# Group 1's keys and queries: four loads of four tokens a packet on half the partitions each, or two loads of two tokens a packet on all of them

## The chip, the cores and the metric

The kernel runs on one core of a Trainium2 chip. A core has a matrix engine (TensorE, PE in the profile), a vector engine (DVE), a scalar engine (ACT), a GpSimd engine (POOL) and a sync engine (SP), which work side by side and wait for one another by semaphores. SBUF is the on-chip memory of 128 partitions; PSUM is the matrix engine's output memory, cut into eight banks. Transfers between the device's main memory (HBM) and SBUF are issued by an engine's queue and carried out by 16 DMA engines. The metric is the device time of one execution in microseconds (us); lower is better.

## The reference

Two stages follow one another. The first is attention with a sliding window of 128 tokens and four sink tokens, for four sequences of 768 tokens, eight heads of 64 features:

```
scores = q @ k^T / 8                    # per sequence and head
keep   = (k_pos < 4) | (0 <= q_pos - k_pos < 128)
a      = softmax over the kept scores
x      = a @ v                          # put together to 3072 tokens x 512 features
```

The second is a gated feed-forward block on the 3072 tokens:

```
g   = x @ w_gate                        # 512 x 1536
out = (g * sigmoid(g) * (x @ w_val)) @ w_out   # 1536 x 512
```

The inputs and the output are float32; the kernel calculates in bfloat16 and adds up in float32.

## The kernel before, in words

The tokens are cut into twelve groups of 256, three to a sequence (`GC`). For each group the kernel brings keys and queries into SBUF, turns them so that the features lie on the partitions (`kTs` and `qTs`: head pair by head pair, 64 features of an even head above 64 of an odd one, tokens along the row), multiplies them to scores, takes exponentials on ACT, masks on DVE, multiplies with the values, divides by the sums, turns the result into `xT`, and feeds it to the feed-forward block. The attention of a later group is laid between the feed-forward products of an earlier one.

The order of the work on each engine is the order of the program's text: the schedule is written out by hand (`tc.manual_schedule()`), and every engine carries out its own instructions in that order. Nothing is planned by cost. What is moved in the text moves on its engine's queue.

How keys and queries get turned depends on the group. Group 0 comes in by two ways at once: heads 0 to 3 as float32 by the queues of SP and ACT (`st`, line 205) and then cast, heads 4 to 7 by POOL's queue, which casts on the way (`x0`, line 216). In `x0` each partition holds two neighbouring tokens of a head (`by_two`, line 198). Group 1, the one that the change touches, comes by four loads of POOL's queue (`load_rows`, line 97). Each takes 64 partitions: a partition holds four neighbouring tokens (`by_rows`, line 86, "r=4"), the even heads of the four pairs lie on partitions 0 to 63 and the odd ones on 64 to 127. So each load has 64 x 4 packets of 4 x 64 elements. Later groups come by whole token rows (`load_nat`).

The next work on POOL's queue, in the program's order, are the values of groups 0 and 1 (`va`, line 151, four loads), the first gate and value weights (`wg`, `wv`, line 162), and three small copies. All of these loads share the 16 DMA engines.

`step_T` (line 252) turns group 1 on the matrix engine. A matrix product with an identity matrix turns 64 tokens x 64 features. It uses a quarter of the array: partitions 0 to 63 give columns 0 to 63 (an even head), partitions 64 to 127 give columns 64 to 127 (an odd head), in turn. One call handles two head pairs with 16 such products into one PSUM bank; there are four calls, two for the keys and two for the queries (lines 820 to 823). After its 16 products each call copies its bank to `kTs` or `qTs`, on ACT or on DVE, and puts the four interleaved tokens back in order. The third call, the queries of pairs 0 and 1, is copied by DVE (line 271); the other three are copied by ACT (line 269).

Then come, on the matrix engine, the first eight products with group 0's values (`step_PV`, line 494), the scores of group 1 for pairs 0 and 1 (`step_S`, line 326), 16 more products with values, the scores of pair 2, the sinks' scores (line 432), the turning of group 0's result (line 543), the scores of pair 3, and then the first feed-forward product (`pg`, line 564). `step_S` for pairs 0 and 1 multiplies the second half of group 0's keys with the first half of group 1's queries first, then the first half of group 1's keys with all its queries, and last the second half with the second half.

Of the kernel before, what the change touches and what calls it, by code (L numbers as in the profile page):

```python
# [7 lines left out]
FP32 = mybir.dt.float32  # L8
BF16 = mybir.dt.bfloat16
# [5 lines left out]
def kernel(  # L15
# [12 lines left out]
    nc = tc.nc  # L28
    P = 128
    B, H, S, D = q.shape  # L30
# [8 lines left out]
    NP2 = H // 2  # L39
# [15 lines left out]
    def pool(name, bufs, psum=False):  # L55
        if psum:
            return ctx.enter_context(
                tc.tile_pool(name=name, bufs=bufs, space=bass.MemoryType.PSUM))
        return ctx.enter_context(tc.tile_pool(name=name, bufs=bufs))
# [3 lines left out]
    rowp = pool("rowp", 3)  # L63
# [16 lines left out]
    def bank(shape, dtype, name):  # L80
        return psum.tile(shape, dtype, tag="b", name=name)


    rows, nats, vas = {}, {}, {}

    def by_rows(src, b, w, pairs, t0):

        hs = slice(2 * pairs.start + w, 2 * pairs.stop, 2)
        return src[b, hs, t0:t0 + 256].rearrange("p (m r) d -> m p (r d)", r=4)

    ALL = slice(0, NP2)

    def new_rows(g):
        rows[g] = rowp.tile([P, 2, NP2, 4 * D], BF16, tag="rows", name="rows")
        return rows[g]

    def load_rows(g, i):
        b, c = divmod(g, GC)
        if g not in rows:
            new_rows(g)  # L100
        for w in range(2):
            nc.gpsimd.dma_start(  # L102
                rows[g][64 * w:64 * (w + 1), i],
                by_rows((k, q)[i], b, w, ALL, c * 256))

    def load_nat(g):
        b, c = divmod(g, GC)
# [65 lines left out]
    ident = const.tile([P, P], BF16)  # L173
# [21 lines left out]

    def by_two(src, h0, n=4):
        return src[0, h0:h0 + n, 0:256].rearrange("h (m r) d -> m h (r d)", r=2)

    x0 = const.tile([P, 2, H, 2 * D], BF16)
    st = [rowp.tile([P, H, 2 * D], FP32, tag="rows", name="st") for _ in range(2)]
    for h0 in (0, 2):
        for i, eng in ((0, nc.sync), (1, nc.scalar)):
            eng.dma_start(st[i][:, h0:h0 + 2], by_two((k, q)[i], h0, 2))
# [9 lines left out]
    for i in range(2):  # L215
        nc.gpsimd.dma_start(x0[:, i, 4:8], by_two((k, q)[i], 4))  # L216
    nc.gpsimd.iota(tq, [[1, P]], base=0, channel_multiplier=0,
                   allow_small_or_imprecise_dtypes=True)
    nc.gpsimd.iota(tk, [[0, 1]], base=0, channel_multiplier=1,
                   allow_small_or_imprecise_dtypes=True)  # L220
    load_rows(1, 0)
    load_rows(1, 1)
    load_v(0)
    load_v(1)
# [6 lines left out]
    kTs, qTs, es_t, e_t, xns, xTs = {}, {}, {}, {}, {}, {}  # L231
# [15 lines left out]
    def new_T(b):  # L247
        if b not in kTs:
            kTs[b] = kqtp.tile([P, NP2, S], BF16, tag="kT", name="kT")
            qTs[b] = kqtp.tile([P, NP2, S], BF16, tag="qT", name="qT")  # L250

    def step_T(g, i, p2, evict=None):
        b, c = divmod(g, GC)
        new_T(b)
        x = rows[g]
        pt = bank([P, 2, 256], FP32, "pt")
        for pp in range(2):
            p = 2 * p2 + pp
            for r in range(4):
                for w in range(2):  # L260
                    h = slice(64 * w, 64 * (w + 1))
                    nc.tensor.matmul(
                        pt[h, pp, 64 * r:64 * (r + 1)], x[h, i, p, r * D:(r + 1) * D],
                        ident[h, h], start=True, stop=True, skip_group_check=True)
        dst = (kTs, qTs)[i][b][:, 2 * p2:2 * p2 + 2, c * 256:(c + 1) * 256].rearrange(
            "q a (m r) -> q a m r", r=4)
        pt = pt.rearrange("q a (r m) -> q a m r", r=4)
        if (evict or ("a", "v")[i]) == "a":
            nc.scalar.copy(out=dst, in_=pt)
        else:  # L270
            nc.vector.tensor_copy(out=dst, in_=pt)

    def step_TN(g, i, j, evict="av"):

# [542 lines left out]
    load_sinks(vcl, 1, B)  # L817
    build_maskq()

    step_T(1, 0, 0, "a")  # L820
    step_T(1, 0, 1, "a")
    step_T(1, 1, 0, "v")
    step_T(1, 1, 1, "a")
    step_PV(0, 0, 0)
    step_PV(0, 0, 1)
    flush()
# [98 lines left out]
```

## Time and profile before

| | |
|---|---|
| median of three timed runs | 234.06 us (233.25 to 235.14) |
| the profiled execution's own time | 233.82 us |
| its span, first to last instruction | 231.9 us |
| PE busy | 225.6 us, 97% of the span |
| DVE, ACT, POOL busy | 150.9, 106.4, 84.3 us |
| DMA queue of POOL | 79,904 packets, 14.29 MB |
| all packets; those under 512 bytes | 112,008; 99,056 |

The span is what the profile's rows cover; the own time is 1.9 us more, from what lies before the first and after the last instruction. Times in the rows are counted from the span's start. A row of the profile names an engine, a line of the kernel and the tile written and read; the time in square brackets is how long the engine sat idle before it and what it waited for. "Landing" of a load is the time from its issue to the arrival of its last byte. The page also gives the clock that the matrix engine was granted, in tenths of its full speed.

### The profile page before, as it was taken

Reading aid. Unit: us, or ns where it says so; the run is one execution under the profiler, and the core shown is the slowest. Engines: PE = TensorE matmul, PEld = TensorE weight load, DVE = VectorE, ACT = ScalarE, POOL = GpSimd, SP = SyncE. Lnnn points to the kernel's source line nnn. Section 1 sums busy time; section 2 is a strip of 40 time slices with the busy share of each in tenths; the row PEclk is TensorE's granted clock in tenths of the full one; section 3 lists DMA queues with packets and bytes.
Section 4 is the critical chain, followed back from the end, with each engine's and each line's share of the span. In section 5 each row is a group of like instructions: output and inputs, shape, how many; then the busy total and the mean of one; then the engine's idle time right before and its main releaser. Section 6 shows DMA issues by size and latency. Waiting matters only on the chain.

```text
span 231.9 us, 5433 instructions
## 1 busy us (share of the span) xinstructions
PE 225.6 (97%) x2155; PEld 125.4 (54%) x2155; DVE 150.9 (65%) x327; ACT 106.4 (46%) x212; POOL 84.3 (36%) x123
## 2 busy tenths in 40 slices
PE   7699999999999999999999999999999999999994
PEld 3469645796555644455444454454454544487443
DVE  5878888767660797960797970597960599778000
ACT  4784486566543726423635512835612823333221
POOL 8996874960500907806353415135000000000000
PEclk9979999999999999999999999999999999999999
DMA  8999999999998998998989996989915102000132
GB/s 147 150 185 179 179 198 206 164 156 122 123 154 230 103 134 99 151 195 141 146 119 139 128 124 138 105 109 144 117 40 144 45 3 42 3 3 0 64 120 90
DMA packets 112008, 28.04 MB, mean 121 GB/s; under 512 B 99056, under 2 KB 109040, under 8 KB 111984
## 3 DMA queue, kind: packets, MB, share of 16 engines
q0 software_dynamic: 79904, 14.29, 80.7%
q1 hardware_dynamic: 30672, 11.58, 26.7%
q10 hardware_dynamic: 1408, 1.84, 2.5%
q8 instruction: 17, 0.28, 0.5%
q14 instruction: 7, 0.06, 0.1%
HBM read 29.13 MB, written 6.29 MB: 153 GB/s over the span
## 4 chain that ended last, share of the span: by engine, by line
PE 94%; DMA 2%; POOL 2%; DVE 0%; issue 0%; POOLq 0%
PE pg L564 27%; PE pv L564 27%; PE pd L657 27%; PE o L494 4%; PE s L382 3%; DMA rows<-in_q_dram 2%; PE s L326 1%; PE o L463 1%; PE pk L432 1%; PE pn L279 1%; PE o L454 1%; POOL rows L102 1%; POOL x L216 1%; PE px L543 1%; DVE xT L550 0%
## 5 line engine op out<-in xcount | busy, mean ns | idle before, releaser
L592 DVE SCALAR_TENSOR_TENSOR u<-th,pg 128x512 bf16<-128x512 f32 x72 | 49.2, 683 | 45.4 <-ACT th L584 45.1
L564 PE MATMUL pg<-xT,wg 128*128 128x512 bf16 (+1 forms) x360 | 74.2, 337 | 0.3 <-DVE xT L550 0.3
L564 PE MATMUL pv<-xT,wv 128*128 128x512 bf16 (+1 forms) x360 | 74.1, 336 | 0.0
L584 ACT ACTIVATE th<-pg 128x512 f32<-128x512 f32 x72 | 43.7, 608 | 59.6 <-PE pg L564 59.6
L657 PE MATMUL pd<-wo,ht 128*128 128x512 bf16 (+2 forms) x300 | 65.9, 370 | 0.0
L564 PEld LDWEIGHTS <-wg 128*128 128x128 bf16 x360 | 34.4, 98 | 26.7 <-issue 0.7
L564 PEld LDWEIGHTS <-wv 128*128 128x128 bf16 x360 | 33.9, 98 | 23.5 <-issue 0.2
L607 DVE TENSOR_TENSOR ht<-u,pv 128x512 bf16<-128x512 bf16 x62 | 42.5, 686 | 4.7 <-PE pv L564 0.4
L657 PEld LDWEIGHTS <-ht 128*128 128x128 bf16 x300 | 27.5, 98 | 28.4
L662 ACT ACTIVATE ot<-pd 128x512 f32<-128x512 f32 (+1 forms) x24 | 14.3, 595 | 50.2 <-PE pd L657 46.8
L395 ACT ACTIVATE e<-s 128x512 bf16<-128x512 f32 x54 | 28.5, 614 | 5.8 <-PE s L382 4.9
L113 POOL DMA_DIRECT2D nat<-in_k_dram x20 | 17.7, 895 | 29.3 <-DMA qT<-nat 27.8
L511 DVE TENSOR_TENSOR xn<-o,rcp 128x256 bf16<-128x256 f32 x45 | 17.9, 419 | 0.7
L128 POOL DMA_DIRECT2D vm<-in_v_dram x24 | 17.8, 770 | 1.2 <-DMA va<-in_v_dram 0.7
L113 POOL DMA_DIRECT2D nat<-in_q_dram x20 | 17.8, 906 | 1.0 <-DMA wv<-in_moe_w_val_dram 0.5
L494 PEld LDWEIGHTS <-e 128*128 128x128 bf16 x256 | 12.0, 100 | 6.3 <-issue 0.3
L404 DVE TENSOR_TENSOR e<-e,maskq 128x768 bf16<-128x768 bf16 x24 | 13.1, 553 | 1.9 <-ACT e L395 1.9
L151 POOL DMA_DIRECT2D va<-in_v_dram x12 | 10.7, 917 | 4.3 <-DMA wo<-in_moe_w_out_dram 2.4
L703 POOL CAST warmed<-xT 1x1 f32<-1x1 bf16 x3 | 0.5, 175 | 30.2 <-DMA xT<-xn 30.2
L503 DVE RECIPROCAL rcp<-o 128x4 f32<-128x4 f32 x48 | 7.3, 172 | 5.5 <-PE o L494 5.3
L664 DVE TENSOR_SCALAR ot<-pd 128x128 f32<-128x128 f32 x1 | 0.3, 292 | 14.3 <-PE pd L657 14.3
L333 ACT ACTIVATE e<-s 128x512 bf16<-128x512 f32 x16 | 8.3, 607 | 0.6 <-PE s L326 0.5
(86 smaller groups left out, 138.7 us busy)
## 6 DMA issues: line engine op xcount, KB each, us to landing
out_dram<-ot SPq DMA_DIRECT2D x17, 256.0 KB
nat<-in_k_dram POOLq DMA_DIRECT2D x20, 128.0 KB, 4.7
nat<-in_q_dram POOLq DMA_DIRECT2D x20, 128.0 KB, 4.9
va<-in_v_dram POOLq DMA_DIRECT2D x12, 128.0 KB, 5.9
wg<-in_moe_w_gate_dram POOLq DMA_DIRECT2D x6, 256.0 KB, 7.6
wv<-in_moe_w_val_dram POOLq DMA_DIRECT2D x6, 256.0 KB, 8.2
wo<-in_moe_w_out_dram POOLq DMA_DIRECT2D x4, 384.0 KB, 11.1
out_dram<-ot ACTq DMA_DIRECT2D x6, 256.0 KB
```

The source lines that it names most:

```text
L113: nc.gpsimd.dma_start(x[:, i, j].rearrange("p (h d) -> p h d", d=D), src[b, :, t0:t0 + P].rearrange("h p d -> p h d"))
L128: nc.gpsimd.dma_start(vms[b][p0:p1, t - 1, :, 0:D], v[b, :, t0:t0 + p1 - p0].rearrange("h p d -> p h d"))
L395: nc.scalar.activation(e_t[g][:, e0:e0 + 512], pss[g][w, i], AF.Exp, scale=scale)
L404: nc.vector.tensor_tensor(e, e, m.broadcast_to([P, 2, 384]), op=ALU.mult)
L494: nc.tensor.matmul(o, l, r, start=(c == 0 and i == 0), stop=(i == len(mms) - 1), skip_group_check=True)
L511: nc.vector.tensor_tensor(xn, po[:, :, 0:D], rcp.broadcast_to([P, 4, D]), op=ALU.mult)
L564: nc.tensor.matmul(ps[:, i * n:(i + 1) * n], ws[fi][:, c, fo * P:(fo + 1) * P], xTs[tb][:, c], start=(c == 0), stop=(c == DMC - 1))
L584: nc.scalar.activation(th, pg, AF.Tanh, scale=0.5)
L592: nc.vector.scalar_tensor_tensor(u, th, 1.0, pg, op0=ALU.add, op1=ALU.mult)
L607: nc.vector.tensor_tensor(hts[tb][:, f:f + 512 // SIZES[tb]].rearrange("p a n -> p (a n)"), u, pv, op=ALU.mult)
L657: nc.tensor.matmul(po, hts[tb][:, f, ts * P:(ts + 1) * P], wos[f // n][:, f % n, lo:hi], start=(f == 0), stop=(f == DFC - 1))
L662: nc.scalar.activation(ot, po, AF.Copy, scale=0.5)
```

## The change

Group 1's keys now come by one load and its queries by one. A partition holds two neighbouring tokens of all eight heads, with `by_two`, which has been made general and takes the place of `by_rows`: 128 x 8 packets of 2 x 64 elements a load. The bytes are the same.

With this layout, partitions 0 to 63 hold the first 128 tokens of the group and 64 to 127 the second 128, for even and odd heads alike. `step_T` takes all four head pairs in one call, and is called once for the keys and once for the queries. Its 32 products go in turn to the four quarters of the array; the first 128 tokens write one PSUM bank and the second 128 another. After all 32 products, each bank is copied: both banks of the keys by ACT, the first bank of the queries by DVE and the second by ACT. The number of products and of copies, and the size of a copy (128 x 512), are as before.

```diff
-    def by_rows(src, b, w, pairs, t0):
-        hs = slice(2 * pairs.start + w, 2 * pairs.stop, 2)
-        return src[b, hs, t0:t0 + 256].rearrange("p (m r) d -> m p (r d)", r=4)
+    def by_two(src, h0, n=4, b=0, t0=0):
+        return src[b, h0:h0 + n, t0:t0 + 256].rearrange("h (m r) d -> m h (r d)", r=2)
...
-        for w in range(2):
-            nc.gpsimd.dma_start(
-                rows[g][64 * w:64 * (w + 1), i],
-                by_rows((k, q)[i], b, w, ALL, c * 256))
+        nc.gpsimd.dma_start(rows[g][:, i, h0:h0 + n],
+                            by_two((k, q)[i], h0, n, b, c * 256))
...
-    def step_T(g, i, p2, evict=None):
+    def step_T(g, i, evict="av"):
...
-        pt = bank([P, 2, 256], FP32, "pt")
-        for pp in range(2):
-            p = 2 * p2 + pp
-            for r in range(4):
-                for w in range(2):
-                    h = slice(64 * w, 64 * (w + 1))
+        pts = [bank([P, NP2, P], FP32, "pt") for _ in range(2)]
+        for p in range(NP2):
+            for r in range(2):
+                for a, w in ((0, 0), (1, 1), (0, 1), (1, 0)):
+                    ha = slice(64 * a, 64 * (a + 1))
                     nc.tensor.matmul(
-                        pt[h, pp, 64 * r:64 * (r + 1)], x[h, i, p, r * D:(r + 1) * D],
-                        ident[h, h], start=True, stop=True, skip_group_check=True)
+                        pts[a][64 * w:64 * (w + 1), p, 64 * r:64 * (r + 1)],
+                        x[ha, i, 2 * p + w, r * D:(r + 1) * D], ident[ha, ha],
+                        start=True, stop=True, skip_group_check=True)
+        for a in range(2):
+            t0 = c * 256 + P * a
+            dst = (kTs, qTs)[i][b][:, :, t0:t0 + P].rearrange("q a (m r) -> q a m r", r=2)
+            pt = pts[a].rearrange("q a (r m) -> q a m r", r=2)
+            if evict[a] == "a":
+                nc.scalar.copy(out=dst, in_=pt)
+            else:
+                nc.vector.tensor_copy(out=dst, in_=pt)
...
-    step_T(1, 0, 0, "a")
-    step_T(1, 0, 1, "a")
-    step_T(1, 1, 0, "v")
-    step_T(1, 1, 1, "a")
+    step_T(1, 0, "aa")
+    step_T(1, 1, "va")
```

More of the change, by code (lines that the diff above doesn't have):

```diff
@@ L84, with load_rows @@
     rows, nats, vas = {}, {}, {}
-    def by_rows(src, b, w, pairs, t0):
-        hs = slice(2 * pairs.start + w, 2 * pairs.stop, 2)
-        return src[b, hs, t0:t0 + 256].rearrange("p (m r) d -> m p (r d)", r=4)
-    ALL = slice(0, NP2)
+    def by_two(src, h0, n=4, b=0, t0=0):
+        return src[b, h0:h0 + n, t0:t0 + 256].rearrange("h (m r) d -> m h (r d)", r=2)
     def new_rows(g):
-        rows[g] = rowp.tile([P, 2, NP2, 4 * D], BF16, tag="rows", name="rows")
+        rows[g] = rowp.tile([P, 2, H, 2 * D], BF16, tag="rows", name="rows")
         return rows[g]
-    def load_rows(g, i):
+    def load_rows(g, i, h0=0, n=8):
         b, c = divmod(g, GC)
@@ L194 @@
     nc.vector.memset(kss, 0.0)
-    def by_two(src, h0, n=4):
-        return src[0, h0:h0 + n, 0:256].rearrange("h (m r) d -> m h (r d)", r=2)
     x0 = const.tile([P, 2, H, 2 * D], BF16)
@@ L255, in step_T @@
         x = rows[g]
-        pt = bank([P, 2, 256], FP32, "pt")
-        for pp in range(2):
-            p = 2 * p2 + pp
-            for r in range(4):
-                for w in range(2):
-                    h = slice(64 * w, 64 * (w + 1))
-                    nc.tensor.matmul(
-                        pt[h, pp, 64 * r:64 * (r + 1)], x[h, i, p, r * D:(r + 1) * D],
-                        ident[h, h], start=True, stop=True, skip_group_check=True)
[L265 to L271, printed above, removed]
+        pts = [bank([P, NP2, P], FP32, "pt") for _ in range(2)]
[3 more added lines that the diff above has]
+                    ha = slice(64 * a, 64 * (a + 1))
+                    nc.tensor.matmul(
+                        pts[a][64 * w:64 * (w + 1), p, 64 * r:64 * (r + 1)],
[9 more added lines that the diff above has]
+                nc.vector.tensor_copy(out=dst, in_=pt)
     def step_TN(g, i, j, evict="av"):
```

## The prediction

> **What bounds the kernel now.** I read the chain of work that ended last first, cut to the first 16 us, since the change touches only the start.
>
> ```profile
> 3.33 1.74 POOL rows L102 x3
> 5.07 5.42 DMA rows<-in_q_dram
> 10.49 0.04 issue
> 10.54 0.69 PE pt L262 x31
> 11.23 0.06 issue
> 11.29 0.51 PE o L494 x8
> 11.80 0.99 PE s L326 x12
> ```
>
> The columns are start, length and what it was. The queries' second load lands at 10.49 us; from there the chain is the matrix engine, and the page gives it 94% of the whole span, with gaps of tenths of a microsecond after 16 us. So whatever moves the first score product (line 326, now at 11.75 to 11.80) moves the end by the same amount, unless something else is late next.
>
> Second, the instructions in order of time around that point:
>
> ```profile
> 10.54 0.69 PE L262 MATMUL pt<-ident,rows 64*64 64x64 bf16 x31 [0.78 <-DMA rows<-in_q_dram]
> ...
> 11.01 0.69 DVE L271 CAST qT<-pt 128x512 bf16<-128x512 f32 x1 [0.81 <-PE pt L262]
> ...
> 11.26 0.59 ACT L269 CAST qT<-pt 128x512 bf16<-128x512 f32 x1 [0.84 <-PE pt L262]
> ...
> 11.75 1.04 PE L326 MATMUL s<-qT,kT 64*128 64x128 bf16 x12
> ...
> 15.57 0.10 PEld L564 LDWEIGHTS <-wg 128*128 128x128 bf16 x1 [0.16 <-DMA wg<-in_moe_w_gate_dram]
> ```
>
> The matrix engine idles 0.78 us for the queries' second load, and 0.31 us before that for their first. DVE's copy begins at 11.01, in the middle of the products, because pairs 0 and 1 have their own bank; it ends at 11.70, just as the scores begin. The first gate weights are waited for until 15.57, close behind the work that uses them.
>
> Third, the stretches of the load phase, with the bytes that moved (last column, GB/s):
>
> ```profile
> 3.90:5.10 1.20, 1.17 (x16) 0.60 (x16) 1.20 (x6) 0.80 (x3) 1.20 (x3) 1.00 1.62 159
> 5.30:7.30 2.00, 1.48 (x27) 0.87 (x25) 1.90 (x6) 1.67 (x5) 2.00 (x3) 1.00 1.24 125
> 7.40:8.40 1.00, 0.95 (x10) 0.42 (x10) 1.00 (x3) 0.67 (x3) 1.00 (x3) 1.00 1.29 161
> 9.80:11.20 1.40, 0.66 (x31) 0.58 (x31) 0.58 (x4) 0.62 (x2) 1.31 (x4) 1.00 2.42 154
> 13.80:15.00 1.20, 1.20 (x20) 0.70 (x21) 0.82 (x3) 1.20 (x4) 1.14 (x2) 0.57 1.44 194
> ```
>
> They hold, in this order, mostly group 0's `x` (two tokens a packet, all partitions: the shape that the change brings), group 1's keys, its queries, the values, the gate weights. The queue never runs dry, so the landing of the queries is set by this rate. The keys' stretch is the slow one.
>
> Fourth, the clock. The granted clock is halved once, from about 11.42 to 14.84 us; cut at those edges:
>
> ```profile
> 8.01:11.42 3.41, 2.26 (x74) 1.71 (x74) 2.55 (x8) 2.57 (x7) 3.28 (x7) 1.00 2.08 164
> 11.42:14.84 3.42, 3.42 (x53) 2.39 (x51) 2.21 (x9) 2.89 (x6) 3.35 (x6) 0.50 1.73 175
> ```
>
> The stretch before the halving was 66% busy on the matrix engine (2.26 of 3.41); in the halved one the engine was busy throughout (3.42 of 3.42).
>
> **The change part by part.**
>
> *Issue.* Four loads of 0.65 us on POOL (rows L102: 0.649 to 0.670) become two of 1,024 packets. The values' loads have that count, 128 x 8, and take 0.90 us (va L151, median 0.905). So 2.6 us become 1.8, and POOL reaches everything behind them 0.8 us earlier. That is worth nothing by itself: every load waits its turn in a queue that is full (`va` is issued at 5.67 and lands some 5.5 us later). The cover is the backlog. Were it gone, 0.8 us would be the gain.
>
> *Transfer.* 1,024 packets of 512 bytes become 2,048 of 256, with the same 0.524 MB. Before: 2.0 us at 125 GB/s move 0.25 MB, the other 0.274 MB at about 160 take 1.71 us, together 3.71. The nearest row for the new shape is `x`, at 159: 0.524 / 0.160 = 3.28 us, a gain of 0.43. If the slow rate belongs to the moment and lasts the whole transfer, 0.524 / 0.125 = 4.19, a loss of 0.48. At the weights' 194 it would be 2.70, a gain of 1.01. I take 0.43, by the row of the same shape and source, and keep -1.01 to +0.48. The queries then land at 10.06.
>
> The Trainium skill, "DMA: Bandwidth & Descriptors", section Specifications, speaks against this: it asks for at least 512 bytes a transfer to reach line rate. Taken as an estimate that a 256-byte packet costs what a 512-byte one does, the 3.71 us would double and the start would come 3.7 us later. The `x` row, 256-byte packets at 159 GB/s against 125 to 161 for the 512-byte rows, does not bear that out here, so the sum goes without it.
>
> *Products.* 64 before and after. The 31 of the queries take 0.69 us, of which 0.19 is one product's own length (rows, matmul: median 193 ns), so they start over 0.50. Now two quarters work at a time. The nearest row for four at a time is the sinks' products, line 454, four strips in 0.29 us together. With four the 0.50 would be 0.25, with no more overlap than now it stays. I take no gain (0 to -0.25): consecutive products alternate halves as they do now.
>
> *Copies.* The same four, 128x512. But a bank is now ready only when all 32 products are. The keys have over a microsecond of cover before the queries land (ACT copies them from 9.32 to 10.43); without it, 0.25 us late. The queries have none: DVE's copy started 0.25 us before ACT's (11.01 against 11.26) and now starts with it. With products at 10.10 to 10.79, both copies start at about 10.83; ACT ends at 11.42, DVE at 11.52. The scores wait for both halves, so for DVE: they start at about 11.58, 0.06 after it as now.
>
> *What lies between.* The eight products with values wait for `va`, whose landing moves with the rows. At 0.03 us each at full clock they fit between 10.9 and 11.3, so their queue place before the scores costs nothing. The matrix engine then idles some 0.3 us, a new wait, with everything on that engine queued behind it.
>
> **Sum**: -0.43 (landing) + 0.25 (copy starts with the last product) = -0.18 at the scores (11.75 to 11.58). Behind it the engine is busy through the halved stretch, so the 0.18 stays to the first `pg`; the weights land 0.43 earlier too. From the profiled execution's 233.82 that is 233.65. The median of the runs shown is 0.24 above the profiled one; I forecast 233.7. Bounds of the pieces: -1.01 - 0.25 + 0.25 = -1.0, and +0.48 + 0.25 = +0.7.
>
> **The rivals.**
>
> 1. *The copy's wait takes the place of the load's wait, and more.* Place: the scores behind DVE's copy of the queries' first half. Price: 0.25 us, plus up to 0.48 of transfer. It decides from a landing after 10.24 (10.49 - 0.25). For it: the first products, the copies and the scores stand in one line without cover. Against it: the stretch at 159. Result 233.9 to 234.55, about 234.3.
>
> 2. *The halved clock goes.* If the queries land early enough that the stretch 8.01 to 11.42 fills up (the stretch before it, 4.60 to 8.01, is 80% busy at 2.72 of 3.41 and was followed by full clock), the next 3.4 us run at full speed. The gain is not all of the 1.7 us: the first gate weights land at 15.57 less 0.43, so `pg`, at 15.94 now, can move to about 15.1. Result about 233.0. Against it: with fewer or faster products the share hardly rises; 0.43 us of earlier work adds about 0.15 us of value products, for 66 to 70%.
> The Trainium skill, "TensorE: Matmul & The Clock Gate", Part 1, says that this activity window runs freely against the program; if so, its place differs from run to run, which one trace cannot show.
>
> 3. *The change does not speed the transfer*, and the quicker products give back what the copy loses: four quarters at a time save 0.25, the copy costs 0.25. Result 233.8.
>
> **How the numbers follow.** Forecast 0.47, rival 1 0.25, rival 2 0.16, rival 3 0.12. The range runs from rival 2 less the spread of the runs before (0.8 below their median): 232.2, to rival 1's upper end 234.55 on the median's basis (+0.24) plus the same doubt: 235.1. One per cent, about what a measurement of this kernel can tell from no change, is 2.34 us: under 231.7 or over 236.4. Only rival 2 with every bound on its side, or a second halved stretch (a busy 3.4 us at half clock costs 1.7) on top of rival 1, gets there: 0.04 and 0.04.
>
> **What would show it.** Two rows on line 98 of about 0.9 us each. 1,024 more packets less 32 completion ones: 113,000, of which 101,072 under 512 bytes. The queries landing at 9.9 to 10.2; the keys' stretch at 155 or more. DVE's and ACT's copies of the queries starting within 0.05 us of each other, the scores 0.7 to 0.8 after the last turning product. A landing after 10.3 makes rival 1; no 0.5 in the clock makes rival 2. I am wrong if the end moves by more than the scores' start does, or if the slow stretch is still there.

## The result, and the profile after

Timed beside each other in 22 executions each, the kernel before took 233.29 us (median; 232.68 to 235.14) and the changed kernel 234.32 us (233.46 to 236.52). The ratio is 1.0043, with a 95% interval of 1.0025 to 1.0061: the change costs about 1.0 us, where the forecast was a gain of a few tenths. It is less than one per cent, as was given a chance of 0.92, and on the side of the first rival. An execution more than 1.5% above the fastest of its kernel counts as slow: the ratios in this document are of the other executions, the medians of all.

The profiled execution of the changed kernel took 235.32 us, its span is 233.3 us (before: 233.82 and 231.9). These lines of its page answer the step on issue and packets, and the clock:

```profile
PEclk9959999999999999999999999999999999999999
DMA packets 113000, 28.04 MB, mean 120 GB/s; under 512 B 101072, under 2 KB 110032, under 8 KB 112976
```

The packets are the predicted 113,000 and 101,072. The clock's third slice now holds a 5 where the page of before has a 7: there is more time at half clock than before.

The chain of work that ended last, cut to the same stretch as before (start, length, what):

```profile
5.02 7.02 DMA va<-in_v_dram
12.04 0.14 issue
12.17 0.60 PE o L488 x8
12.77 0.97 PE s L320 x12
```

The values stand where the queries' second load stood, and the scores come at 12.71 to 12.77 instead of 11.75 to 11.80. The values are not a new bound of their own: they lie behind the queries in the same full queue. The instructions in order of time show both (start, length, engine, line; in brackets the idle time before and its releaser):

```profile
4.15 0.90 POOL L98 DMA_DIRECT2D rows<-in_q_dram  x1
...
9.71 0.45 PE L254 MATMUL pt<-ident,rows 64*64 64x64 bf16 x32 [1.11 <-DMA rows<-in_k_dram]
...
11.22 0.64 PE L254 MATMUL pt<-ident,rows 64*64 64x64 bf16 x32 [1.06 <-DMA rows<-in_q_dram]
...
11.91 0.69 DVE L265 CAST qT<-pt 128x512 bf16<-128x512 f32 x1 [1.56 <-PE pt L254]
11.94 0.58 ACT L263 CAST qT<-pt 128x512 bf16<-128x512 f32 x1 [0.66 <-PE pt L254]
12.17 0.60 PE L488 MATMUL o<-va,e 128*128 128x65 bf16 x8 [0.31 <-DMA va<-in_v_dram]
...
12.71 1.04 PE L320 MATMUL s<-qT,kT 64*128 64x128 bf16 x12
...
17.10 1.07 PE L558 MATMUL pg<-xT,wg 128*128 128x256 bf16 x6
```

The queries are waited for until 11.22, and landed at 11.18 instead of 10.49: 0.69 us later, not 0.43 earlier. From the landing to the scores it takes 1.53 us instead of 1.26. That is not the later copy alone, though it is near the predicted 0.25: the queries' products ran at half clock here (0.64 us, where the keys' took 0.45), and the scores stand behind value products that waited for `va`. From the scores to the first gate product (`pg`) it takes 4.39 instead of 4.19. Together `pg` starts 1.16 us later (15.94 to 17.10), and the span is 1.4 us longer.

The same stretches of the load phase as were cut before (third last column the granted clock, last the GB/s):

```profile
3.90:5.10 1.20, 0.76 (x10) 0.25 (x8) 1.20 (x5) 0.78 (x3) 1.20 (x3) 1.00 1.39 136
5.30:7.30 2.00, 1.85 (x33) 1.12 (x33) 1.96 (x8) 1.52 (x6) 2.00 (x3) 1.00 1.46 140
7.40:8.40 1.00, 0.80 (x9) 0.39 (x9) 1.00 (x4) 0.84 (x4) 1.00 (x2) 1.00 1.65 162
```

Look at the first row. It holds mostly group 0's `x`, which the change doesn't touch, and which the prediction took as its price for the new shape: 136 GB/s now, 159 before. A load that is the same in both kernels moves by 15% from one execution to another. A difference of that size between two rows of one trace says nothing yet about two shapes.

Last, the clock, cut at its own edges in this execution:

```profile
10.83:14.24 3.41, 2.71 (x63) 2.15 (x64) 1.69 (x5) 1.94 (x4) 3.17 (x5) 0.50 1.98 176
14.24:17.66 3.42, 3.42 (x40) 2.17 (x38) 2.48 (x8) 2.83 (x8) 3.16 (x5) 0.50 1.45 194
```

Two stretches of 3.41 us at half clock, from 10.83 to 17.66, where before had one (11.42 to 14.84). The first of them was 79% busy (2.71 of 3.41) and the half clock went on.

### The profile page after: what moved, and what is told of

It reads as the page before. It is cut to its first block, busy times and chain, and to the rows that moved or that the text cites. A ratio compares the mean times of both kernels' runs of the same rounds, so it can differ in the third digit from the quotient of the medians.

```text
span 233.3 us, 5428 instructions
## 1 busy us (share of the span) xinstructions
PE 225.6 (97%) x2155; PEld 125.1 (54%) x2155; DVE 151.4 (65%) x327; ACT 106.7 (46%) x212; POOL 83.5 (36%) x121
## 2 busy tenths in 40 slices
DMA packets 113000, 28.04 MB, mean 120 GB/s; under 512 B 101072, under 2 KB 110032, under 8 KB 112976
## 4 chain that ended last, share of the span: by engine, by line
PE 94%; DMA 3%; POOL 2%; issue 0%; DVE 0%; POOLq 0%
PE pg L558 27%; PE pv L558 27%; PE pd L651 27%; PE o L488 4%; PE s L376 3%; DMA va<-in_v_dram 3%; PE s L320 1%; PE o L457 1%; PE pk L426 1%; PE px L537 1%; PE pn L273 1%; PE o L448 1%; POOL rows L98 1%; POOL x L208 1%; DVE ot L658 0%
```

## The experiments

Three causes stood against each other: the **loads** (they arrive later, or take more of the queue, in the new shape), the **copies** (both wait for all 32 products), and the **clock** (the new start falls into two stretches at half clock). A further question came up on the way: what the loss passes through to reach the end.

All ratios are to the kernel before, run beside it on the same chip.

| kernel | median us | ratio, 95% interval | executions |
|---|---|---|---|
| the changed kernel again | 234.86 | 1.0035, 1.0004 to 1.0066 | 10 |
| changed, loads in halves | 233.86 | 1.0007, 0.9975 to 1.0040 | 12 |
| the same, a second time | 235.28 | 1.0081, 1.0059 to 1.0103 | 6 |
| before, copies late | 233.27 | 0.9980, 0.9950 to 1.0009 | 12 |
| the same, a second time | 234.09 | 1.0024, 0.9998 to 1.0051 | 12 |
| changed, two quarters at a time | 234.44 | 1.0022, 0.9993 to 1.0050 | 12 |
| changed, loads by half the partitions | 234.31 | 1.0026, 1.0000 to 1.0052 | 12 |
| before, one load a tensor on 64 partitions | 234.62 | 1.0032, 1.0002 to 1.0062 | 12 |
| before, gate weights ahead of values | 233.65 | 0.9999, 0.9971 to 1.0027 | 12 |
| changed, gate weights ahead of values | 234.44 | 1.0032, 0.9999 to 1.0065 | 12 |
| before, 0.13 MB more ahead of the keys | 234.47 | 1.0037, 1.0011 to 1.0063 | 12 |
| before, 0.13 MB more behind the values | 233.93 | 1.0017, 0.9990 to 1.0044 | 12 |
| changed, zero products at the loads | 235.10 | 1.0046, 1.0018 to 1.0073 | 12 |
| before, zero products at the queries | 236.85 | 1.0121, 1.0072 to 1.0170 | 6 |
| before, zero products at two places | 235.66 | 1.0049, 1.0017 to 1.0081 | 12 |
| changed, zero products at two places | 234.48 | 1.0053, 1.0033 to 1.0074 | 6 |
| one load a tensor, zero products at two places | 235.70 | 1.0100, 1.0060 to 1.0141 | 6 |
| half the partitions, zero products at two places | 236.11 | 1.0104, 1.0056 to 1.0152 | 6 |

Two of these kernels were measured a second time, on another chip, and their ratios differ by 0.4 and 0.7 per cent between the two times; the changed kernel gave 1.0043 and 1.0035. So a single ratio here may be off by about half a per cent, whatever its interval says, and only what several of them agree on is used below.

### The changed kernel again

> The changed kernel once more, for a second look at the landings. Theory T (the shape of the loads): the keys land after 9.3 us and the queries after 10.8 again, with one or two DMA engines far behind the rest. Theory L (one execution's bad luck with a DMA engine): the keys land before 8.8 and the queries before 10.5, and the time lost comes from the copies and the clock.

Measured: 1.0035, so the loss is there again. Its profile went another way, though. The clock stayed full (from 6.20 on), the queries landed at 10.31, and the span is 231.7. The chain that ended last:

```profile
8.49 7.15 DMA wg<-in_moe_w_gate_dram
15.64 0.05 issue
15.69 1.05 PE pg L558 x8
```

And the queries on their way to the scores, now at full clock:

```profile
10.35 0.45 PE L254 MATMUL pt<-ident,rows 64*64 64x64 bf16 x32 [1.01 <-DMA rows<-in_q_dram]
10.86 0.69 DVE L265 CAST qT<-pt 128x512 bf16<-128x512 f32 x1 [0.16 <-PE pt L254]
11.67 0.61 PE L320 MATMUL s<-qT,kT 64*128 64x128 bf16 x12
```

From the landing, DVE's copy starts after 0.55 us and the scores after 1.36; in before these were 0.52 and 1.26. The 32 products take 0.45 us with four quarters in turn, where 31 took 0.69 before, and so the copy that waits for all of them starts hardly later.

The matrix engine was early, waited for the first gate weights until 15.64 (before: 15.40 landed, 15.57 used), and the end follows from there. The path to the end is therefore not "queries, scores, and everything behind" alone. It is `pg`, and `pg` starts at the later of two: the matrix engine's own chain, or the landing of weights which lie behind group 1's loads in a full queue. From the start of `pg` on, the profiles agree: 216.0 us to the end of the span in before (15.94 and 231.9) and in this one (15.69 and 231.7); 216.2 in the first profile of the changed kernel (17.10 and 233.3), where the half clock lasted 0.56 us into `pg`.

### The copies alone

This is the kernel before, whose products go in turn to both banks, so that both are ready only after 32. Loads and layout are as before.

```diff
-        for pp in range(2):
-            p = 2 * p2 + pp
-            for r in range(4):
-                for w in range(2):
+        for pp in range(2):
+            for r in range(4):
+                for p2 in range(2):
+                    p = 2 * p2 + pp
+                    for w in range(2):
```

> The kernel before, loads untouched, but the products of a tensor's two banks taken in turn, so that both banks are ready only after all 32: the copies' part of the change alone. The prediction's step says +0.25 us at the first score product and at the end. Theory T says that this is the smaller part of the 1.0 us lost, 0.2 to 0.3. Theory L says that it is nearly all, with the clock: 0.6 to 1.0.

> The kernel before with only the copies' part of the change (both banks ready after all 32 products), a second time: the first gave 0.998 with an interval of 0.995 to 1.0009. If the prediction's +0.25 us for the later copy reaches the end, the ratio is 1.001 or more; if the gate weights' landing covers it, 0.998 to 1.000 again.

Measured: 0.9980 and 1.0024. Against the kernel before beside them, the means are 0.3 us lower and 0.5 higher. Over the 24 executions of both times the mean is 233.79, against 233.61 over the 131 of the kernel before: 0.2 us of the 1.0, with an uncertainty of about 0.3. By what was written ahead of the second one, 1.001 or more would say that the copy's 0.25 us reach the end, and the first one says that they don't; the two together decide neither. The instructions of the first of them show a wait for the copy:

```profile
12.08 0.62 PE L328 MATMUL s<-qT,kT 64*128 64x128 bf16 x12 [0.17 <-DVE qT L273]
```

It is not the mark of the late copy: the kernel before with its gate weights moved ahead (below), whose copies are early, has the same wait there (0.18). In this execution it doesn't reach the end, since `pg` waits for something else:

```profile
9.18 5.86 DMA wg<-in_moe_w_gate_dram
15.04 0.05 issue
15.09 1.05 PE pg L566 x8
```

The second execution, of the same kernel, had its weights at 16.10 instead of 15.04. Identical loads land up to 1.1 us apart, so no single profile can show a shift of a few tenths.

### Two quarters at a time

This is the changed kernel, with the 16 products of the first 128 tokens ahead of the other 16. Its first bank is ready early again, and only two quarters work side by side.

```diff
-        for p in range(NP2):
-            for r in range(2):
-                for a, w in ((0, 0), (1, 1), (0, 1), (1, 0)):
+        for a in range(2):
+            for p in range(NP2):
+                for r, w in ((0, 0), (0, 1), (1, 0), (1, 1)):
```

> The changed kernel with the 16 products of the first token half ahead of the 16 of the second: the first bank is ready after 16. The loads are as changed; two quarters of the same rows work at a time in place of four. The first copy starts 0.2 us earlier against the second. Theory T: the median stays 0.6 or more above the kernel before. Theory L: it comes back to within 0.3 of it.

Measured: 1.0022, and 234.47 as a mean, 0.9 over the 131 and 0.7 over the kernel before beside it. The interval, 0.9993 to 1.0050, just reaches no change; as it stands, most of the loss stays when the copies are early and the quarters work in another order. In its profile `pg` waits for the gate weights until 16.51.

One thing must be read with care here. The page of this execution has full clock in every slice, and its recorded mean clock is 1.0, but its products are longer than those of the changed kernel's first profile. One and the same product of zeros, there and here:

```profile
7.87 0.39 PE L724 MATMUL s<-zero 128*128 128x512 bf16 x1
```

```profile
8.59 0.61 PE L724 MATMUL s<-zero 128*128 128x512 bf16 x1
```

The 32 products of the keys took 0.88 us here, and that is a price at half clock, not one of two quarters. The trace has the change to full clock at 14.05; what lies ahead of the first such change is not counted as half clock by the page or the mean. In the other profiles of this document the products of zeros at the start are as slow, and full clock comes between 3.9 and 7.1 us, save with the first fill in the changed kernel (below): 10.52.

### The shape and the number of the loads

First, the changed kernel with each of its loads in two halves by heads (four loads again; the packets stay at two tokens, on all partitions):

```diff
-    load_rows(1, 0)
-    load_rows(1, 1)
+    for i in range(2):
+        for h0 in (0, 4):
+            load_rows(1, i, h0, 4)
```

> The changed kernel with each of the two loads cut into heads 0 to 3 and heads 4 to 7: four loads of 128 x 4 packets, the same packets. Theory T by packets (256 bytes are slow here): nothing changes against the changed kernel, 0 +- 0.2 us. Theory T by size of a load (1,024 packets at once let one engine fall behind): the queries land 0.4 us or more earlier than in the changed kernel, and the median falls by 0.4 to 0.8. POOL pays 0.8 to 1.0 us more for issuing in both.

> The changed kernel with each load cut into heads 0 to 3 and 4 to 7, a second time: the first gave 1.0007 with an interval of 0.9975 to 1.004, too wide to tell. The packets are those of the changed kernel, only the size of a load differs. By packets: 1.003 to 1.005 like the changed kernel. By load size: 1.002 or less.

Measured: 1.0007, and 1.0081 the second time. Taken together, 18 executions with a mean of 234.64 (234.47 without one of 237.64), it is about as slow as the changed kernel (234.63). That loads in halves repair it, as the first time seemed to say, is not shown.

Second, the changed kernel with its loads cut by token halves instead: four loads of 64 partitions, as before, but with packets of two tokens:

```diff
-        nc.gpsimd.dma_start(rows[g][:, i, h0:h0 + n],
-                            by_two((k, q)[i], h0, n, b, c * 256))
+        for a in range(2):
+            t0 = c * 256 + P * a
+            nc.gpsimd.dma_start(rows[g][64 * a:64 * (a + 1), i],
+                (k, q)[i][b, :, t0:t0 + P].rearrange("h (m r) d -> m h (r d)", r=2))
```

> The changed kernel with each load cut by the token halves: four loads of 64 partitions, 64 x 8 packets of 256 bytes. Theory W (new, from the first runs): the start is set by the landing of the first gate weights behind group 1's loads, and the change lost time because these now land later. Of why they land later: by packets (256 bytes move at 155 to 165 GB/s, 512 bytes at 175 to 195 where nothing disturbs them) this kernel stays as slow as the changed one, 0.5 to 1.0 us over the kernel before; by load size or by partitions (64 partitions are better) it comes back to within 0.3 of the kernel before.

Third, the kernel before with packets of four tokens, but one load a tensor, on 64 partitions; the products read their rows from partitions 0 to 63 alone:

```diff
-        for w in range(2):
-            nc.gpsimd.dma_start(
-                rows[g][64 * w:64 * (w + 1), i],
-                by_rows((k, q)[i], b, w, ALL, c * 256))
+        nc.gpsimd.dma_start(rows[g][i],
+            (k, q)[i][b, :, c * 256:(c + 1) * 256].rearrange("h (m r) d -> m h (r d)", r=4))
```

> The kernel before with one load a tensor: 64 partitions, each with four tokens of all eight heads, 64 x 8 packets of 512 bytes; the products read partitions 0 to 63 only. By packets: within 0.3 us of the kernel before. By load size: 0.5 to 1.0 over it, like the changed kernel.

Measured: 1.0026 and 1.0032. Small packets in the old number of loads lose, and large packets in the new number of loads lose as well, by 0.6 and 0.8 us as means. Each of the four ways of loading that is not before's costs between 0.6 and 1.0 us. Which property does it, packet or number, these runs don't separate: by what was written ahead, the second kernel speaks for the packets and the third for the size of a load.

What of the queue differs can be seen in the stretch 5.50 to 8.50, in which group 1's loads move. Of the changed kernel, in the first run and again, and of the kernel with late copies, whose loads are before's:

```profile
5.50:8.50 3.00, 2.55 (x40) 1.33 (x34) 2.96 (x10) 2.54 (x7) 3.00 (x5) 1.00 1.54 149
```

```profile
5.50:8.50 3.00, 2.54 (x38) 1.27 (x34) 2.67 (x10) 2.26 (x7) 3.00 (x5) 1.00 1.41 135
```

```profile
5.50:8.50 3.00, 1.81 (x30) 0.97 (x29) 2.33 (x8) 1.69 (x5) 3.00 (x5) 1.00 1.44 177
```

And of the kernel before itself, whose trace the prediction went by:

```profile
5.50:8.50 3.00, 2.34 (x35) 1.28 (x34) 2.96 (x10) 2.34 (x7) 3.00 (x5) 1.00 1.21 136
```

In the nine profiles with packets of four tokens this column reads 136, 177, 163, 171, 160, 153, 157, 173 and 157 (mean 161); in the ten with two tokens 149, 135, 142, 143, 142, 154, 128, 158, 152 and 148 (mean 145). The profile with the extra load ahead of the keys (below) is left out, since that load moves in this stretch. The kernel before's own profile is the lowest of its kind. In the stretch 5.30 to 7.30 itself, the six other profiles with before's loads read 146 to 169, so the 125 GB/s that the prediction wanted to repair were a sample of that one execution, not the price of the shape. But a rate is not yet a loss: the kernel with one load a tensor on 64 partitions reads 173 and 157 here, and its queries land at 10.94 and 11.24, later than in any of the seven profiles with before's loads (9.97 to 10.69).

### Whether a delay of the queue reaches the end

The kernel before with one load more, of 0.13 MB into a tile that nothing reads: once ahead of group 1's keys, once behind the values of group 1 (just ahead of the gate weights).

```diff
+    extra = const.tile([P, 4, 2 * D], BF16)
...
+    nc.gpsimd.dma_start(extra, by_two(k, 0))
```

> The kernel before with one more load ahead of group 1's: 512 packets of 256 bytes, 0.13 MB, into a tile that nothing reads; at 160 GB/s 0.8 us of the queue. It prices a delay of everything behind: if the start hangs on the transfers one to one, +0.8 us at the end; if the matrix engine's own chain covers some of it, 0.2 to 0.5.

> The same extra load, but behind the values of group 1 and ahead of the first gate weights: the queries land as before, the weights 0.8 us later. Theory W (the weights' landing): +0.5 to +0.8 us. Theory Q (the landing of keys and queries, with the clock): 0 to +0.2.

Measured: 1.0037 and 1.0017, as means 0.9 and 0.7 us over before (0.13 MB at 160 GB/s is 0.8 us; the second mean holds one execution of 237.03 and is 0.5 over without it). The first one's `pg`:

```profile
16.26 1.05 PE L566 MATMUL pg<-xT,wg 128*128 128x256 bf16 x8 [0.96 <-DMA wg<-in_moe_w_gate_dram]
```

In both profiles `pg` waits for the gate weights. Time spent ahead of them in this queue passes on to the end: of 0.8 us, 0.3 to 1.5 by the first interval. The second interval reaches from 0.9990 to 1.0044, so for that place alone it is likely, not certain.

### The gate weights ahead of the values

If the weights are late, they can go first: the loads of the first gate and value weights move ahead of the values of group 1, once in the kernel before, once in the changed one.

```diff
     load_v(0)
-    load_v(1)
     load_gate(0)
+    load_v(1)
```

> The kernel before with the first gate and value weights issued ahead of group 1's values. Theory W: the weights land some 1.7 us earlier and the end moves up by as much as the matrix engine then has no other wait for: 0.3 to 1.0 us less than before. Rival (the queries' landing and the chain behind it set the start): no change within 0.2, or later by what group 1's values then wait.

> The changed kernel with the same move. Theory W: it gains more than the kernel before does, 0.8 to 1.5 us, and the distance between the two shrinks to 0.3 or less. Rival (the queries' landing): the distance stays at 0.8 to 1.0.

Measured: 0.9999 and 1.0032; neither gains. In the changed one `pg` did start at 14.34, and then the wait is for the values that were put back:

```profile
16.15 0.40 PE L488 MATMUL o<-va,e 128*128 128x65 bf16 x8 [0.42 <-DMA va<-in_v_dram]
16.98 0.37 PE L488 MATMUL o<-va,e 128*128 128x65 bf16 x7 [0.43 <-DMA va<-in_v_dram]
```

The rest of its span is 217.2 us instead of 216.0. So here the wait moved from the weights to the values. In the kernel before with the same move `pg` started at 14.83 and no such wait shows; its span is 231.2, and yet the median of its 12 executions is no lower. That the sum of the bytes ahead bounds the stretch, and not their order, fits both, but isn't shown.

### The clock

The mean granted clock is on record for every execution. One stretch of 3.41 us at half clock takes 1.7 us off 232, which makes 0.993, and two make 0.985. So the executions can be sorted by how many stretches they had, as far as the record counts them (from the first change to full clock on):

| kernel | none counted: executions, median us | one | two or more |
|---|---|---|---|
| before (131) | 80, 233.22 | 50, 233.86 | 1, 234.40 |
| copies late (24) | 16, 233.25 | 5, 234.18 | 3, 235.30 |
| changed (32) | 8, 234.88 | 16, 234.07 | 8, 235.34 |
| changed, loads in halves (18) | 8, 233.54 | 7, 235.29 | 3, 236.20 |
| changed, by half the partitions (12) | 1, 234.83 | 7, 233.83 | 4, 234.31 |
| one load a tensor, 64 partitions (12) | 1, 233.22 | 5, 233.68 | 6, 235.05 |

Two stretches came once in 131 executions of the kernel before, and in 8 of 32 of the changed one. With one stretch counted, the changed kernel and the two ways of loading in the last rows lie within about 0.2 us of before (234.07, 233.83 and 233.68 against 233.86): much of their loss sits in the executions with two. Loads in halves don't fit this (235.29 with one). And the changed kernel is slow with none counted as well (234.88 against 233.22; its eight executions lie between 233.64 and 235.97). Whether these had a late first full clock, like the two profiles that show one at 14.05 and 10.52, is not on record.

To take the clock out, the matrix engine was kept busy where it waits for loads, by products of zeros into banks that the real products then overwrite: two ahead of the keys' products and four ahead of the queries' in the changed kernel, four ahead of the queries' in the one before.

```diff
         pts = [bank([P, NP2, P], FP32, "pt") for _ in range(2)]
+        fill((2, 4)[i], pts[0].rearrange("p a x -> p (a x)"), 512)
```

> The changed kernel with idle products of zeros, 128 x 512, in the two waits of the matrix engine: two ahead of the keys' products, four ahead of the queries', into the bank that the products then overwrite. They keep the engine busy where it waits for group 1. Theory C (the later keys leave the engine idle, and it loses a second half-clock stretch): the runs with a granted clock of 0.985 and less go, and the median falls by 0.3 to 0.6. Theory W: the engine then waits longer for the weights, change under 0.2.

> The kernel before with four such products ahead of the queries'. Theory C: its runs at 0.993 become runs at full clock, and the median falls by 0.2 to 0.4. Theory W: under 0.2.

Then three of them ahead of the queries' products and three ahead of the first `pg`, with four ways of loading:

```diff
+        if i == 1:
+            fill(3, pts[0].rearrange("p a x -> p (a x)"), 512)
...
+        if name == "pg" and tb == 0 and f == 0:
+            fill(3, ps, 512)
```

> The kernel before with three idle products of zeros ahead of the queries' products and three ahead of the first gate product, so that neither wait leaves the matrix engine idle for long. In all runs so far the span is the first gate product's start plus 216.0 us, save where a half-clock stretch falls behind that start (217.5 in one). Theory C (idling ahead of the weights puts the half-clock stretch into the dense work and makes the runs above 235): none above 235, median 232.9 to 233.4. Rival (those runs have another cause): they stay, about one in six.

> The changed kernel with the same two fills. If the change's loss is the clock's, the distance to the kernel before with fills falls to 0.3 us or less; if it is the queue's, it stays at 0.6 to 1.0 with the clock full in nearly all runs.

> One load a tensor with 512-byte packets on 64 partitions, with the fills. By packets: within 0.3 us of the kernel before with fills. By load size: as far from it as the changed kernel with fills.

> Four loads of 256-byte packets on 64 partitions each, with the fills. By packets: as far from the kernel before with fills as the changed kernel with fills. By load size: within 0.3 us of the kernel before with fills.

Measured: no kernel got faster. With the first fill 9 of 12 executions of the changed kernel have no half clock counted, and these had a median of 234.40; but the profile is one of them, and its first full clock came at 10.52. With two fills all six have none counted (the profile is at full clock from 5.16 on), and it took 234.48. That would say that the half clock is not what the changed kernel loses by, or not alone. But the fills also brought a loss of their own, to the kernel before most of all (236.85). Where it may lie shows in the profile of the kernel before with two fills and of the changed one with two, one row each, of the scores of a later group whose queries and keys are turned by transfers:

```profile
75.78 1.49 PE L384 MATMUL s<-qT,kT 64*64 64x192 bf16 x52 [2.89 <-DMA qT<-nat]
```

```profile
74.75 0.89 PE L378 MATMUL s<-qT,kT 64*64 64x192 bf16 x52 [1.83 <-DMA qT<-nat]
```

In the first of the two rows the products ran at half clock, which came at 75.57, at the end of the wait. There is a second place, at 74 us, where transfers can end last; neither the kernel before nor the changed one waits there in its own profile. The fills made this measurement useless for what it was meant for. Why they delay those transfers is open, and whether the changed kernel's executions at full clock wait there too is open as well.

## Why the prediction was wrong

**Issue, packets:** right. Two rows on line 98 of 0.94 and 0.90 us, 113,000 packets, and no gain from POOL's earlier issues.

**Transfer:** this is the step that failed: "The nearest row for the new shape is `x`, at 159: 0.524 / 0.160 = 3.28 us, a gain of 0.43", and with it "The queries then land at 10.06". They landed at 10.49 on the mean of the six profiles of the changed kernel's loads (10.07 to 11.18), and at 10.39 in seven of the old loads (9.97 to 10.69). The price of the new shape wasn't far off; two tokens a packet move at 145 GB/s on the mean of ten profiles. What was wrong is the price of the old shape: 125 to 136 in that one profile, 161 on the mean of nine. There was nothing to gain. Worked out again from the means, 0.524 MB take 3.61 us at 145 against 3.25 at 161: a loss of 0.36, nearer to the bound of +0.48 that was kept than to the -0.43 that was taken. The landings show less of it: the queries 0.10 later, and the first gate weights 0.25 (15.63 on the mean of five profiles of the changed kernel's loads in their old place, 15.38 in five of the old), where profiles of the same loads lie up to 1.5 us apart. So it is shown that the gain didn't come, and not how large the loss of the transfer is.

The Trainium skill, "DMA: Bandwidth & Descriptors", section Specifications, asks for at least 512 bytes a transfer for line rate. The direction agrees with the rates here, 145 GB/s for 256-byte packets and 161 for 512-byte ones. The page doesn't say how much is lost below; the prediction's estimate from it, twice the time, was far too high: a tenth, if the difference is the packets' at all.

**Products:** mis-sized. The prediction took no gain (0 to -0.25), and four quarters do work at a time: 32 products in 0.45 us, where two at a time take 0.69 for 31. That is the 0.24 at the far end of its range.

**Copies:** both copies start within 0.03 us of each other, as said. But the term of +0.25 held only with slow products. At full clock the products give back what the copy loses: in the changed kernel's second profile DVE's copy starts 0.55 us after the landing instead of 0.52, and the scores 1.36 instead of 1.26. That is the mechanism of rival 3, priced as it was there; that nothing would be lost by the transfer, and its 233.8, are not borne out. Whether the later copy by itself moves the end stays open: 24 executions with late copies alone lose 0.2 us, give or take 0.3.

**The sum:** the forecast of 233.7 isn't what its terms give on the basis that it names (233.65 + 0.24 = 233.9), and the upper end of the range, with the doubt of 0.8 that the lower end has, would be 235.6 and not 235.1. Neither decides anything here.

**The path:** "whatever moves the first score product ... moves the end by the same amount, unless something else is late next" had the exception in its own third quoted row, the gate weights waited for until 15.57. It gave the weights 0.43 of relief by the failed step and so dropped them. They are what the profiles show ahead of `pg` in the changed kernel's second run, with two quarters at a time, with loads in halves (1.57 and 1.74 us of wait in two profiles), with late copies in both, and with the extra load in both places. In the changed kernel's first profile they are not: they landed at 15.90, and `pg` came at 17.10 behind work at half clock. Its own sign of being wrong, "if the end moves by more than the scores' start does", is there: the scores moved by 0.96 us, the span by 1.4.

**The clock:** rival 2 asked whether the half clock would go, and held that a stretch 80% busy is followed by full clock. It was the other way: two stretches in a quarter of the executions. The busy share doesn't decide it: with two quarters at a time the clock stayed at half after stretches of 3.41 us (counted back from 14.05) that were 93% and 88% busy, 3.17 and 3.00 us. The tail that the prediction gave a chance of 0.04, "a second halved stretch ... on top of rival 1", is that quarter; it cost 1.3 us within the changed kernel (235.34 against 234.07) and not enough to pass one per cent.

**Rival 1** named the side, and 234.3. That this meets the measured 234.32 is luck: it was counted from 234.06, the median of three runs, and 22 executions of the same kernel gave 233.29. As a difference it said +0.25, and +0.73 at the most; measured is +1.0. Its place, the copy, is not what the profiles show; its addition, "plus up to 0.48 of transfer", is nearer to it.

What of the 1.0 us is shown: the forecast gain of the transfer didn't come, and a delay in this queue passes to the end. That the loss comes with the loads, and not with the copies or the order of the quarters, is what the runs point to: all four ways of loading that are not before's lose 0.6 to 1.0 us on the mean, and late copies 0.2. No run has the new loads with everything else unchanged, so it is argued, not shown. What stays open: whether packet size or the number and extent of the loads does it; how much goes by later landings, how much by one DMA engine that lags (last section), and how much by half clock, the second stretch or a late start; and why the executions of the changed kernel with no half clock counted are as slow as 234.88, while its one profile of that kind has a span of 231.7 (233.71 as a whole).

No version here is shown to beat both kernels. Late copies gave 0.9980 once and 1.0024 the second time, the weights moved ahead 0.9999.

## What to carry to other kernels

A rate read over one or two microseconds of one trace is a sample: before a gain is built on a slow stretch, look whether an untouched load in the same trace, or the same load in another profile, moves as slowly. Where a queue is full, ask what lies behind the load that is being changed, down to the first instruction that waits for the last of it; the small wait that the page shows there (0.16 us here) may be the next bound. Where a profile says full clock, compare the length of one and the same product with another profile. And when effects are below half a per cent, measure the same kernel a second time before believing an interval.

## What the runs showed of the hardware

- **A load can be held up by the last of its parts, for long.** The trace has 16 marks of completion for each load, read here as one for each of the 16 DMA engines; the load has landed with the last. In the first profile of the changed kernel the ninth mark of the queries came at 9.31 (before: 9.66), the last but one at 10.38 (before: 9.91) and the last at 11.18 (before: 10.49). The last mark was 0.8 us behind the one before it from the keys (9.67 and 8.88) to the gate weights (15.90 and 15.10). What held it up doesn't show. One thing that may: each profile has a packet of 16 KB of instructions between 11 and 15 us that takes one engine 0.94 to 1.35 us, at 11.40, 12.27, 12.93 and 13.87 in four of them. With two quarters at a time it started at 13.99; the two last marks were 0.06 us apart for the values that landed at 14.03, and 1.22 at the first gate weights, for which `pg` waited (16.51 and 15.29).
- **The half clock doesn't need a wholly idle stretch.** It followed a stretch that was 66% busy on the matrix engine (before, 8.01 to 11.42), and it went on after one that was 79% busy, in steps of 3.41 us, and after stretches of 93% and 88% with two quarters at a time. The edges differ between executions of one kernel (10.83 in the changed kernel's first profile, none from 6.20 to 231 in its second).
- **Four quarters of the array work at once** when consecutive products go to different ones: 32 products of 64 x 64 in 0.45 us at full clock, where 31 with two quarters at a time took 0.69.
- **A packet of half the size takes more than half the time.** In the trace of before, a packet of 512 bytes of POOL's queue took a median of 60 ns between 5.5 and 8.5 us, in that of the changed kernel one of 256 bytes 41 ns.
